# Column 0 in centered form through the first GLU group, rstd applied afterwards, and gate slices 0 to 3 loaded as 128 KB pieces over two queues

## The chip, the cores and the metric

The kernel runs on one core of one Trainium2 chip. The metric is the device time of one execution in microseconds; it was about 1.8 us longer than the span of the profile in the runs that were profiled. Every kernel was run several times, and the kernel before was run in the same rounds on the same chip.

## The reference, cut to what matters

```python
xn = _layernorm(x, axis=-1)                       # x: 1 x 2048 x 512, bf16
return x + _A_ref(xn, A_w_r, A_w_i) + _B_ref(xn, B_w_gate, B_w_up, B_w_down)
# _A_ref: irfft2(rfft2(xn) * (w_r + 1j * w_i))
# _B_ref: (gelu(xn @ w_gate) * (xn @ w_up)) @ w_down, 512 -> 1792 -> 512
```

The 2048 rows are 16 "columns" of 128 tokens, and the 1792 hidden units 14 "slices" of 128.

## The kernel before

All operations are handed to a small planner in the kernel, which simulates the engines with assumed durations (the first number of each call) and fixes the order of the instructions on each engine. TensorE runs dummy matmuls, so that its clock comes up, until the first column is normalised and transposed.

```python
def layernorm(c0, n, due, after=(), halves=1):
    ...                                            # bn_stats, bn_aggr, + eps on DVE
    r = add("POOL", 0.55, lambda: nc.gpsimd.tensor_tensor(
        out=rstd[:, k], in0=ve[:, k], in1=half[:, k], op=ALU.pow), (e, o_mem[1]), due - 5, lag=0.1)
    ...                                            # xn = (x - mean) * rstd on DVE, in halves

def pe_transpose(c, due):
    b = _Buf("S")                                  # one PSUM tile for both halves
    ...
        def ev(es=es, eng=(nc.scalar.copy, V.tensor_copy)[h]):   # half 0 on ACT, half 1 on DVE
            eng(out=xnT[c // 4][:, es[0]:es[-1] + 1, c % 4], in_=tiles[f"tp.{c}"][:, es[0]:es[-1] + 1])

load_x(0, 1); d_ident = load_ct("ident", "ident", "ACT"); load_x(1, 1)
load_w(0, 2, ("SP", "ACT"))                        # gate and up slices 0-1, 256 KB each
load_x(2, 2); load_w(2, 4); load_w(4, 6); load_x(4, 4); load_w(6, 10); load_x(8, 4); load_w(10, 14)
...
FIRST = [(0, 1, 0, 4), (1, 1, 0, 4), (0, 2, 4, 2), (2, 2, 0, 2), (2, 2, 2, 2), (2, 2, 4, 2)]
#        column, columns, slice, slices: one PSUM tile g_ps and one u_ps each
```

## Time and profile before

| | before |
|---|---|
| time, median of 6 runs | 179.50 us (179.39 to 180.25) |
| span of the profile | 177.6 us |
| first GLU matmul | 6.89 us |
| clock of TensorE full from | 7.11 us |
| last matmul starts | 174.70 us |
| last DMA landed, end of the span | 176.71, 177.62 us |

### The profile page before, as it was taken

How to read it: one execution, taken by the hardware profiler on the slowest of the kernel's cores; microseconds unless marked ns; L12 is line 12 of the kernel's file. 1: busy time of each engine (PE TensorE's matmuls, PEld its weight loads, DVE VectorE, ACT ScalarE, POOL GpSimd, SP SyncE). 2: the span in 40 equal slices, each digit the busy share in tenths (PEclk: the TensorE clock that was granted, in tenths of full speed). 3: DMA queues.
4: the chain of work that ended last, by engine and by line, in shares of the span. 5: the costliest groups of instructions: out<-in, count | busy, mean ns of one | idle time of the engine just before them, and what ended most of it. 6: DMA issues, size and time to landing. Idle time of an engine off the chain costs nothing.

```text
span 177.6 us, 3041 instructions
## 1 busy us (share of the span) xinstructions
PE 173.4 (98%) x1100; PEld 92.9 (52%) x1100; DVE 118.1 (66%) x266; ACT 87.4 (49%) x158; POOL 18.6 (10%) x33
## 2 busy tenths in 40 slices
PE   6999999999999999999999999999999999999993
PEld 2598545545554544554555455554445444544463
DVE  1869999999537995889999885336442541632522
ACT  3162437456789737999998855453111211211100
POOL 3212138743200000000000000000000000000000
PEclk9999999999999999999999999999999999999999
DMA  5999487999297001302211121100222221322212
GB/s 144 311 355 359 86 270 84 223 296 193 52 347 255 2 0 29 93 2 59 61 48 37 37 59 37 27 0 0 84 68 66 83 89 59 92 80 69 74 45 59
DMA packets 23182, 19.24 MB, mean 108 GB/s; under 512 B 8512, under 2 KB 21824, under 8 KB 23168
## 3 DMA queue, kind: packets, MB, share of 16 engines
q1 hardware_dynamic: 22176, 17.57, 35.0%
q0 software_dynamic: 320, 1.19, 3.1%
q10 hardware_dynamic: 672, 0.30, 0.6%
q8 instruction: 8, 0.13, 0.3%
q14 instruction: 6, 0.05, 0.1%
HBM read 13.28 MB, written 2.10 MB: 87 GB/s over the span
## 4 chain that ended last, share of the span: by engine, by line
PE 91%; ACT 3%; DVE 3%; issue 1%; POOL 0%; DVEq 0%; POOLq 0%
PE u_ps L502 25%; PE g_ps L502 25%; PE warm L380 3%; ACT E L652 2%; PE yp L818 2%; PE bp L581 2%; PE gp L767 2%; PE yp__2078 L872 2%; PE yp__1994 L872 2%; PE yp__1967 L872 2%; PE yp__1936 L872 2%; PE yp__1909 L872 2%; PE yp__1820 L872 2%; PE yp__1793 L872 2%; PE yp__1762 L872 2%; PE yp__1735 L872 2%
## 5 line engine op out<-in xcount | busy, mean ns | idle before, releaser
L502 PE MATMUL g_ps<-xnT,Wg_sb 128*128 128x512 bf16 (+2 forms) x264 | 58.1, 347 | 0.0
L502 PE MATMUL u_ps<-xnT,Wu_sb 128*128 128x512 bf16 (+2 forms) x264 | 57.9, 347 | 0.0
L527 DVE TENSOR_TENSOR hT<-u_ps,ge 128x512 bf16<-128x512 f32 x56 | 38.4, 685 | 17.5 <-PE u_ps L502 14.4
L519 ACT ACTIVATE ge<-g_ps 128x512 bf16<-128x512 f32 x56 | 33.5, 598 | 30.5 <-PE g_ps L502 26.5
L502 PEld LDWEIGHTS <-Wu_sb 128*128 128x128 bf16 x264 | 24.3, 98 | 22.3 <-DMA Wu_sb<-in_B_w_up_dram 0.2
L502 PEld LDWEIGHTS <-Wg_sb 128*128 128x128 bf16 x264 | 24.3, 98 | 20.7 <-issue 0.2
L872 PEld LDWEIGHTS <-hT 128*128 128x128 bf16 x252 | 23.0, 98 | 21.9
L824 ACT CAST yf<-yp 128x512 bf16<-128x512 f32 x16 | 9.3, 586 | 37.6 <-PE yp L818 37.6
L652 ACT CAST E<-ep 64x512 bf16<-64x512 f32 x32 | 18.5, 579 | 1.1 <-PE ep L646 0.7
L396 DVE BATCH_NORM_STATS2 st<-x_t 128x6 f32<-128x512 bf16 x16 | 10.5, 676 | 4.8 <-DMA x_t<-in_A_x_dram 4.8
L629 ACT CAST ds<-dp 128x512 bf16<-128x512 f32 x16 | 8.8, 589 | 1.1 <-PE dp L624 1.0
L773 ACT CAST Gs<-gp 128x512 bf16<-128x512 f32 x16 | 8.6, 593 | 1.0 <-PE gp L767 1.0
L406 POOL TENSOR_TENSOR rstd<-ve,half 128x2 f32<-128x2 f32 (+2 forms) x7 | 6.6, 949 | 21.9 <-DVE ve L404 21.9
L585 ACT CAST Bs<-bp 128x512 bf16<-128x512 f32 x16 | 8.3, 603 | 0.5 <-PE bp L581 0.5
L818 PEld LDWEIGHTS <-Gs 128*128 128x128 bf16 x64 | 4.8, 98 | 3.5
L380 PE MATMUL warm<-warm 128*128 128x512 bf16 (+1 forms) x14 | 5.1, 539 | 1.3 <-POOL half L373 1.3
L412 DVE TENSOR_SCALAR xn<-x_t,mv,rstd 128x512 bf16<-128x512 bf16 (+1 forms) x17 | 6.1, 399 | 0.3 <-POOL rstd L406 0.3
L818 PE MATMUL yp<-CT,Gs 128*128 128x128 bf16 x64 | 6.0, 219 | 0.0
L683 DVE TENSOR_TENSOR m<-X,TW 128x1024 bf16<-128x1024 bf16 x8 | 5.5, 692 | 0.2
L624 PEld LDWEIGHTS <-Bs 128*128 128x128 bf16 x64 | 4.4, 98 | 2.4
L689 DVE TENSOR_TENSOR m<-X,TW 128x1024 bf16<-128x1024 bf16 x8 | 5.5, 684 | 0.0
L646 PE MATMUL ep<-ds,CT 128*128 128x512 bf16 x16 | 5.4, 379 | 0.0
(103 smaller groups left out, 169.0 us busy)
## 6 DMA issues: line engine op xcount, KB each, us to landing
y<-in_A_x_dram SPq DMA_DIRECT2D x16, 128.0 KB, 2.1
F<-F SPq DMA_DIRECT2D x32, 64.0 KB, 2.0
out_dram<-y SPq DMA_DIRECT2D x15, 128.0 KB, 1.7
Wd_sb<-in_B_w_down_dram SPq DMA_DIRECT2D x2, 896.0 KB, 8.3
x_t<-in_A_x_dram SPq DMA_DIRECT2D x3, 512.0 KB, 6.8
Wg_sb<-in_B_w_gate_dram SPq DMA_DIRECT2D x2, 512.0 KB, 6.8
Wu_sb<-in_B_w_up_dram SPq DMA_DIRECT2D x2, 512.0 KB, 9.1
Wg_sb<-in_B_w_gate_dram SPq DMA_DIRECT2D x3, 256.0 KB, 5.1
```

The costliest lines, as they stand in the source:

```text
L380: nc.tensor.matmul(tiles["warm"][:, 0:w], lhsT=warm[:, 0:P], rhs=warm[:, 0:w], start=True, stop=True)
L396: V.bn_stats(out=st[:], in_=x_t[:, c])
L502: nc.tensor.matmul(tiles[f"{nm}.{key}"][:, f * w:f * w + w], lhsT=W[:, e, (f0 + f) * P:(f0 + f + 1) * P], rhs=rhs(e), start=(f + e == 0), ...
L519: nc.scalar.activation(out=e[:, 0:nf * w], in_=tiles[f"g_ps.{key}"][:, 0:nf * w], func=AF.Gelu_apprx_tanh)
L527: V.tensor_tensor(out=out, in0=tiles[f"u_ps.{key}"][:, 0:nf * w].rearrange("p (f w) -> p f w", w=w) if nf > 1 else tiles[f"u_ps.{key}"][:, ...
L585: nc.scalar.copy(out=o, in_=tiles[f"bp.{cg}.{q}"][:].rearrange("p c (r g a) -> p (c r) g a", r=2, a=4))
L629: nc.scalar.copy(out=ds[:].rearrange("p (s k t) -> p s k t", s=2, t=2), in_=tiles[f"dp.{G}"][:].rearrange("p s t k -> p s k t"))
L652: nc.scalar.copy(out=tiles[f"E.{g}"][64 * h:64 * h + 64, r], in_=tiles[f"ep.{g}.{h}"][64 * r:64 * r + 64])
L773: nc.scalar.copy(out=o, in_=tiles[f"gp.{g}.{h}"][:].rearrange("p q (n a) -> p (q n) a", a=4))
L818: nc.tensor.matmul(yp[:, q], lhsT=tiles["G"][:, q, c], rhs=IQ[q], start=(q == 0), stop=(q == 3), skip_group_check=True)
L824: nc.scalar.copy(out=tiles[f"yf.{c // 2}"][:, c % 2], in_=tiles[f"yp.{c}"][:])
L872: nc.tensor.matmul(y[:, s], lhsT=tiles[sb, f][:, cl * P:(cl + 1) * P], rhs=Wd_sb[:, f, s], start=(f == 0), stop=False)
```

## The change

Its intent is to start the first GLU group before rstd of column 0 is known. The centered x - mean is transposed and multiplied, and the PSUM result is scaled by rstd afterwards. For this rstd must lie along the free axis, so one FP32 matmul of ones with diag(rstd) spreads it. The statistics of columns 1 and 3 move from DVE to ACT (sums by accumulator), to make room on DVE. Each half of a transposed column gets its own PSUM tile. The loads are re-cut with longer rows, and one rule of the planner changes.

```diff
-                    at = max([d.end + d.lag + self.HOP for d in o.deps if d.eng != "PE" or o.eng != "PE"] + [0.0])
+                    at = max([d.end + (0.0 if d.eng == o.eng and not d.nbytes else d.lag + self.HOP)
+                              for d in o.deps if d.eng != "PE" or o.eng != "PE"] + [0.0])
 ...
-    load_w(0, 2, ("SP", "ACT"))
+    d_g = [load_first(e, eng) for e, eng in ((1, "ACT"), (0, "SP"), (3, "ACT"), (2, "SP"))]   # gate 0-3, 128 KB each
 ...
+    d_u = load(NE * P * P * 8, lambda: nc.sync.dma_start(out=Wu_sb[:, :, 0:4 * P], in_=wu_v[:, :, 0:4 * P]))
     load_x(2, 2)
-    load_w(2, 4)
-    load_w(4, 6)
+    load_w(4, 8)
 ...
-    NWARM, NGAP, GAP = 10, 1, 4
+    NWARM, GAP = 7, 2
 ...
+    def glu_first(c, f0, nf):      # g_ps and u_ps from the centered column, then on DVE:
+        def scale(k):
+            V.tensor_tensor(out=sc(k), in0=flat(("g_ps", "u_ps")[k]), in1=R(), op=ALU.mult)
 ...
-    FIRST = [(0, 1, 0, 4), (1, 1, 0, 4), (0, 2, 4, 2), (2, 2, 0, 2), (2, 2, 2, 2), (2, 2, 4, 2)]
+    glu_first(0, 0, 4)
+    FIRST = [(1, 1, 0, 4), (0, 2, 4, 2), (2, 1, 0, 4), (3, 1, 0, 4), (0, 2, 6, 2), (2, 2, 4, 2), (2, 2, 6, 2)]
```

## The prediction

> **What bounds the kernel now.** I read the page first, then the busy time of the engines in three stretches, then the start in order of time. The page, its first part and its chain:
>
> ```profile
> span 177.6 us, 3041 instructions
> ...
> PE 173.4 (98%) x1100; PEld 92.9 (52%) x1100; DVE 118.1 (66%) x266; ACT 87.4 (49%) x158; POOL 18.6 (10%) x33
> ...
> PE 91%; ACT 3%; DVE 3%; issue 1%; POOL 0%; DVEq 0%; POOLq 0%
> ```
>
> TensorE is the bound, but a busy PE can hide slow matmuls, so I cut the span at the first GLU matmul and at the end of the last one (columns: stretch, its length, busy time of each engine with instruction counts, granted clock, DMA share, GB/s):
>
> ```profile
> 6.89:174.80 167.91, 167.78 (x1082) 90.78 (x1081) 115.34 (x257) 85.54 (x155) 15.92 (x23) 1.00 0.38 106
> 0.00:6.89 6.89, 5.52 (x18) 2.10 (x19) 2.45 (x9) 1.86 (x3) 2.67 (x10) 1.00 0.68 201
> ```
>
> The middle is a wall: 167.91 us with 0.13 us idle. From start to start a matmul takes 56 ns with 128 columns, 109 ns with 256 and 216 ns with 512 (medians of the trace's 369, 79 and 651 intervals). The wall has 362, 79 and 641 of them: 362 x 0.056 + 79 x 0.109 + 641 x 0.216 = 167.3 us; all its delays, one of 0.28 us at 75.7 and two of 0.2 us near 7.1 and 8.7 among them, make about 0.5 us. So nothing behind the start can be gained but that half microsecond. What is left is the 6.89 us in front of it:
>
> ```profile
> 1.34 4.45 PE L380 MATMUL warm<-warm 128*128 128x512 bf16 x10 [1.34 <-POOL half L373]
> ...
> 3.51 0.69 DVE L396 BATCH_NORM_STATS2 st<-x_t 128x6 f32<-128x512 bf16 x1 [3.51 <-DMA x_t<-in_A_x_dram]
> 4.23 0.18 DVE L403 BATCH_NORM_AGGREGATE mv<-st 128x2 f32<-128x6 f32 x1
> ...
> 4.76 0.58 POOL L406 TENSOR_TENSOR rstd<-ve,half 128x1 f32<-128x1 f32 x1 [2.70 <-DVE ve L404]
> ...
> 5.38 0.60 DVE L412 TENSOR_SCALAR xn<-x_t,mv,rstd 128x256 bf16<-128x256 bf16 x2
> ...
> 6.23 0.63 PE L380 MATMUL warm<-warm 128*128 128x128 bf16 x4
> 6.47 0.37 ACT L431 COPY xnT<-tp 128x256 bf16<-128x256 bf16 x1 [3.29 <-PE tp L428]
> ...
> 6.88 0.29 DVE L431 COPY xnT<-tp 128x256 bf16<-128x256 bf16 x1 [0.83 <-ACT xnT L431]
> 6.89 0.82 PE L502 MATMUL g_ps<-xnT,Wg_sb 128*128 128x128 bf16 x8
> ...
> 8.00 0.39 PE L428 MATMUL tp<-CT,xn 128*128 128x128 bf16 x4
> ```
>
> Here is a serial chain: x lands, statistics, pow on GpSimd, normalise, transpose, copy, first GLU matmul. The two copies of one PSUM tile also run one behind the other (0.83 us of wait in the DVE line).
>
> **What the Trainium skill says.** "TensorE: Matmul & The Clock Gate", section "What's actually happening": an idle TensorE runs at half clock until a free-running window of about 3.4 us has been busy. The trace agrees: the ten dummies span 4.45 us, which is 427 ns apart; four 128-column ones span 0.63 us at 6.23 (107 ns apart) and four transposes 0.39 us at 8.00 (56 ns). The switch to full clock falls at 7.11 us in this run. The section "Wait — 56ns, not 53.3ns?" has 55.6 and 215.7 ns, as here. "FP8 and Floating Point Precision", section "TensorE Precision Notes": true FP32 takes four passes; the new FP32 matmul should then cost about 4 x 56 ns; nothing in before shows it. "DMA: Bandwidth & Descriptors", section "Issuing engines are not separate DMA queues": a second issuing engine saves only issue time. The trace fits: the up piece issued by ACT took 4.2 us to land, those of SP 5.1 to 5.9.
>
> **The change part by part.**
>
> 1. Start. The mean is out at 4.42; centring needs no rstd. By the old spacing (first half 0.35 us, second 0.26 later) the centred halves are ready at 4.80 and 5.06, their transposes start at about 4.85 and 5.11. Each half now has its own PSUM tile: transpose end about 5.24, DVE copy 5.28 to 5.57, first GLU matmul 5.6. The four cold dummies behind the second half (5.30 + 4 x 0.107) end at 5.73, so I take 5.73 instead of 6.89: 1.16 us earlier. The second half's copy (0.37 us on ACT, from about 5.54) is ready for it in time.
> 2. Weights. Gate pieces of 128 KB bring the same 800 KB by the same point as before, when the gate piece landed at 5.85; with 1 KB instead of 512 B rows I put the first two pieces near 4.9 and the others near 5.5. The second half of the gate needs them at about 6.5. The 512 KB up piece: 1312 KB had landed at 7.88 before; at the 356 GB/s of the 9 to 13 us stretch I estimate 7.2, needed at 8.0. Hidden.
> 3. Half clock. The earlier matmuls run before 7.11. From 5.73 to 7.11 some 13 matmuls at 107 ns do what takes 0.72 us warm: 0.66 us lost of the 1.16. Before lost about 0.06. The window is free-running, so this differs from run to run: nothing lost if the clock switches by 5.7, over 1 us if at 8. It may be why one of the three runs of before took 180.25 and the others 179.4 and 179.5.
> 4. More PE work. By the order of the built program the wall has 430 + 1 matmuls of 128 columns, 79 of 256 and 625 of 512. Slices 0-3 of columns 2 and 3 turn from 32 of 256 into 64 of 128 (+0.10 us); slices 6 and 7 of block 0 from 16 of 512 into 32 of 256 (+0.03); column 0 is transposed a second time, behind the first GLU matmuls (+4 x 0.056 = 0.22); the FP32 matmul that spreads rstd (+0.22, perhaps 0.3). Sum +0.6 us.
> 5. Beside it: two scalings of 128x512 out of PSUM (0.69 us each, like hT) and the diagonal on DVE, against the statistics of columns 1 and 3 (0.69 + 0.18 each) that go to ACT as two 0.6 to 0.7 us passes. DVE stays even, and its work is behind PE, which has two PSUM buffers each for gate and up.
> 6. Later: the x load of columns 2 and 3 now follows the up piece (estimate 8.1 instead of 6.73), so normalised columns 2 and 3 come at about 11.1 and 12.0; PE asks for them at 11.6 and 12.7. The three gathers of w_r go ahead of the rstd of columns 4 and 5 on GpSimd: they took 4.8 us with gaps (27.36 to 32.18) before, so from about 11.5 to 16.3. DVE then waits for this rstd with up products queued behind it; their buffer is due to PE at about 19. My estimate of both is 0.1 to 0.3 us of stalls.
>
> Sum: -1.16 + 0.60 (half clock, net) + 0.60 + 0.2 = +0.2 us. Against it the 0.5 us of old delays can partly go: the up weights waited for at 8.8 come earlier, and the order is new, so the 0.28 us at 75.7 may fall out (-0.4 us). With a switch before 7.11, which most phases of a 3.4 us window give, the loss in 3 shrinks to 0.4 on average (-0.2 us). I end at -0.3 to -0.4 us: 179.52 becomes 179.2.
>
> **Rivals.** (a) The start is worth its full 1.2 us: the clock switches early and the stalls vanish. For it: the wall is dense, so a shift of its start moves its end. Against: the 7.11 us of this trace and the counted 0.6 us of work. It would give 178.6. (b) A wait takes the place of the one removed: fewer dummies (7 wide and 6 narrow for 10 and 4) and a hole at 4.5 to 4.85 delay the clock by a window, or DVE, stuck behind the rstd after the gathers, holds an up buffer at 19 us for 0.7 us. For it: DVE is at 2.00 us of 2.00 in the stretches from 14 to 20 us. Against: before too had holes around 5.7 and 6.8 and switched. It would give 180 to 180.5. (c) The gate pieces land late, as small transfers share the 16 engines, and the first matmuls wait up to 0.5 us: largely swallowed by the cold clock; 179.4.
>
> **Range and chances.** The wall cannot shrink, so a gain of 2% (3.6 us) would need the start at about 3.3 us, before x has landed; a loss of 2% needs several new stalls. Both get 1%. The range runs from rival (a) to rival (b): 178.4 to 180.1.
>
> **What would show it.** First g_ps matmul at 5.6 to 5.8; matmuls 107 ns apart up to the switch; one FP32 matmul of 0.2 to 0.3 us; a wall of about 168 us to the last matmul at 174.3 to 174.6. I am wrong if the first GLU matmul is later than 6.3, if PE shows gaps over 0.5 us in sum between 8 and 22 us, or if the last matmul comes before 173.8 or after 175.4.

## More of the kernel before

The studies fell on four chips, on which the kernel before had medians of 179.36, 179.48, 179.28 and 180.07 us, so a kernel is compared with the kernel before of its own rounds.

The prediction shows the page and the start. For the comparison I also cut the span in three (columns: stretch, its length, busy time of each engine with its instructions, granted clock, DMA share, GB/s):

```profile
0.00:15.00 15.00, 13.61 (x126) 9.56 (x127) 8.79 (x24) 5.81 (x10) 3.38 (x11) 1.00 0.91 283
15.00:50.00 35.00, 35.00 (x231) 19.52 (x230) 31.43 (x72) 18.61 (x34) 15.21 (x22) 1.00 0.79 191
50.00:178.00 128.00, 124.80 (x748) 63.80 (x745) 77.86 (x172) 62.98 (x114) 0.00 (x0) 1.00 0.22 65
```

In the middle stretch TensorE, the first number with a count, is busy 35.00 of 35.00 us. So every new wait of TensorE there would lengthen the kernel, and none can be removed.

## The result, and the profile after

The changed kernel took 180.72 us in the median of 6 runs (180.15 to 181.20), against 179.50 us before in the same rounds. The ratio is 1.0059, with a 95% interval of 1.0033 to 1.0086. A ratio here is the mean time of one kernel's runs over that of the other's of the same rounds, so it is not quite the ratio of the medians. For e1 to e16 the ratios come out when the first run of each kernel, the profiled one, is left out. The change is within 2%, as predicted, but the range of 178.4 to 180.1 us is missed, and the sign of the small change is wrong.

The page of the changed kernel (span, busy times, chain by engine):

```profile
span 178.9 us, 3167 instructions
...
PE 173.0 (97%) x1153; PEld 95.0 (53%) x1153; DVE 119.7 (67%) x269; ACT 90.8 (51%) x168; POOL 17.5 (10%) x35
...
PE 73%; DVE 16%; DMA 3%; issue 2%; POOL 2%; SPq 1%
```

TensorE is busy 0.4 us less in a span that is 1.3 us longer, and the chain of waits runs for 16% of the span over DVE and for 3% over DMA, where it had been TensorE for 91%. The same three stretches of the changed kernel:

```profile
0.00:15.00 15.00, 12.69 (x135) 9.67 (x136) 8.89 (x25) 9.02 (x20) 6.26 (x15) 1.00 0.90 296
15.00:50.00 35.00, 34.60 (x269) 20.96 (x266) 33.11 (x73) 17.17 (x32) 11.21 (x20) 1.00 0.77 172
50.00:178.00 128.00, 125.74 (x756) 64.35 (x753) 77.70 (x172) 64.65 (x118) 0.00 (x0) 1.00 0.23 69
```

The idle time of TensorE lies in the first 15 us and, with 0.40 us, in the second stretch. In the last one it is busier only because more work was left. The start of the changed kernel, in order of time:

```profile
4.97 0.29 DVE L497 COPY scr_w<-tm 128x256 bf16<-128x256 bf16 x1 [0.25 <-PE tm L494]
5.10 0.72 ACT L423 ACTIVATE xn<-x_t,sm 128x512 bf16<-128x512 bf16 x1
...
5.32 0.61 PE L578 MATMUL g_ps<-scr_w,Wg_sb 128*128 128x128 bf16 x8
...
5.82 0.35 ACT L497 COPY scr_w<-tm 128x256 bf16<-128x256 bf16 x1
...
6.22 0.61 PE L578 MATMUL g_ps<-scr_w,Wg_sb 128*128 128x128 bf16 x8 [0.29 <-ACT scr_w L497]
...
9.32 0.69 DVE L407 BATCH_NORM_STATS2 st<-x_t 128x6 f32<-128x512 bf16 x1 [1.19 <-DMA x_t<-in_A_x_dram]
...
10.34 0.68 DVE L598 TENSOR_TENSOR scr_b<-g_ps,scr_r 128x512 f32<-128x512 f32 x1
...
11.14 0.78 PEld L630 LDWEIGHTS <-Wg_sb 128*128 128x128 bf16 x8 [0.82 <-DMA Wg_sb<-in_B_w_gate_dram]
11.17 1.03 PE L630 MATMUL g_ps<-xnT,Wg_sb 128*128 128x256 bf16 x8 [0.68 <-DVE scr_b L598]
```

The reader should see four things. The first GLU matmul starts at 5.32 us, 1.57 us earlier than before. Its second half waits for an ACT copy, which stands behind the accumulating passes over column 1 (the second of them at 5.10); this stops TensorE for 0.46 us. And at 9.32 us DVE takes the statistics of column 2, for whose x it has waited 1.19 us; the scaling of g_ps, ready long before, stands behind them in DVE's order. So the first gate buffer comes free at 11.02, and TensorE stops for 0.84 us at 10.3. And the gate slices that it needs next, 4 and 5, come with a load that landed at 10.82 (the PEld line, the weight load). So two waits lie nearly on top of each other: with the buffer free TensorE could have gone on at about 10.87, only some 0.3 us earlier. This is an estimate, from the landing and the 0.05 us that passed in e8_split_dve from a landing at 8.12 to the matmul at 8.17.

To add this up I took, for each matmul, the time to the start of the next and subtracted the spacing of its width (56, 109 or 216 ns, as in the prediction); what is left are the gaps. A small negative sum is rounding of those three numbers. The FP32 matmul, which the trace records twice, is counted as four of 128 columns. The terms add up to the spans:

| us | before | after | difference |
|---|---|---|---|
| start of the first GLU matmul | 6.89 | 5.32 | -1.57 |
| work at the three spacings | 167.30 | 167.87 | +0.57 |
| gaps before 15 us | 0.40 | 1.72 | +1.32 |
| gaps 15 to 50 us | -0.04 | 0.72 | +0.76 |
| gaps after 50 us | 0.14 | -0.10 | -0.24 |
| last matmul start to last DMA landed | 2.01 | 2.01 | 0.00 |
| last DMA landed to end | 0.91 | 1.34 | +0.43 |
| sum | 177.6 | 178.9 | +1.3 |

The gaps of 15 to 50 us are two, in front of and inside the third of the four bp groups, at 44 us. The changed kernel there (several engines):

```profile
39.04 1.38 POOL L433 TENSOR_TENSOR rstd<-ve,half 128x4 f32<-128x4 f32 x1 [11.50 <-DVE ve L415]
...
43.56 0.68 DVE L692 TENSOR_TENSOR xf<-A 128x1024 bf16<-128x1024 bf16 x1
44.16 0.68 DVE L696 TENSOR_TENSOR xf<-A 128x1024 bf16<-128x1024 bf16 x1
...
44.29 0.40 PE L710 MATMUL bp<-RF_t,xf 128*128 128x128 bf16 x4 [0.20 <-DVE xf L692]
44.89 0.84 PE L710 MATMUL bp<-RF_t,xf 128*128 128x128 bf16 x12 [0.20 <-DVE xf L696]
```

TensorE gets xf from DVE at the last moment. The line of GpSimd shows why the planner may have thought it early: pow on 128x4 takes 1.38 us, and the planner has 0.55 us for it.

For the end, the waits of SyncE (waited for: us in total, times, longest); first before, then after:

```profile
SPq L922 <- DMA out_dram<-y: 0.6, 1, 0.6
```

```profile
SPq L1058 <- DMA out_dram<-y: 1.0, 1, 1.0
```

At the end SyncE waits for the completion semaphores of the DMAs in a fixed order, with eight instructions about 62 ns apart. Before, the last store counted on one that the last of them waits for. After, with another number of DMAs, it counts on one of the first, and the seven others follow the landing: 7 x 62 ns is the 0.43 us of the table.

### The profile page after: what moved, and what is told of

It reads as the page before. It is cut to its first block, busy times and chain, and to the rows that moved or that the text cites.

```text
span 178.9 us, 3167 instructions
## 1 busy us (share of the span) xinstructions
PE 173.0 (97%) x1153; PEld 95.0 (53%) x1153; DVE 119.7 (67%) x269; ACT 90.8 (51%) x168; POOL 17.5 (10%) x35
## 3 DMA queue, kind: packets, MB, share of 16 engines
q0 software_dynamic: 320, 1.19, 2.8%
## 4 chain that ended last, share of the span: by engine, by line
PE 73%; DVE 16%; DMA 3%; issue 2%; POOL 2%; SPq 1%
PE u_ps L630 18%; PE g_ps L630 17%; DVE st L407 5%; DVE hT L655 4%; DMA x_t<-in_A_x_dram 3%; DVE xn L439 2%; PE gp L898 2%; PE dp L755 2%; PE yp L954 2%; PE ep L777 2%; PE yp__2122 L1008 2%; PE yp__2095 L1008 2%; PE yp__2064 L1008 2%; PE yp__1979 L1008 2%; PE yp__1948 L1008 2%
## 5 line engine op out<-in xcount | busy, mean ns | idle before, releaser
L630 PE MATMUL g_ps<-xnT,Wg_sb 128*128 128x512 bf16 (+2 forms) x272 | 56.4, 338 | 0.7 <-DVE scr_b L598 0.7
L630 PE MATMUL u_ps<-xnT,Wu_sb 128*128 128x512 bf16 (+2 forms) x272 | 56.4, 338 | 0.0
L655 DVE TENSOR_TENSOR hT<-u_ps,ge 128x512 bf16<-128x512 f32 x55 | 37.5, 683 | 15.3 <-PE u_ps L630 13.4
L647 ACT ACTIVATE ge<-g_ps 128x512 bf16<-128x512 f32 x55 | 33.0, 601 | 28.6 <-PE g_ps L630 27.1
L407 DVE BATCH_NORM_STATS2 st<-x_t 128x6 f32<-128x512 bf16 x14 | 9.4, 674 | 4.4 <-DMA x_t<-in_A_x_dram 4.4
L433 POOL TENSOR_TENSOR rstd<-ve,half 128x1 f32<-128x1 f32 (+2 forms) x7 | 6.1, 865 | 21.4 <-DVE ve L415 19.9
L898 PEld LDWEIGHTS <-F 128*128 128x128 bf16 x64 | 4.2, 98 | 1.9
L439 DVE TENSOR_SCALAR xn<-x_t,mv,rstd 128x512 bf16<-128x512 bf16 x13 | 4.8, 408 | 0.6 <-POOL rstd L433 0.6
L391 PE MATMUL warm<-warm 128*128 128x512 bf16 (+1 forms) x13 | 3.9, 470 | 1.3 <-POOL half L383 1.3
## 6 DMA issues: line engine op xcount, KB each, us to landing
Wu_sb<-in_B_w_up_dram SPq DMA_DIRECT2D x2, 384.0 KB, 10.3
```

The costliest lines, as they stand in the source:

```text
L407: V.bn_stats(out=st[:], in_=x_t[:, c])
L630: nc.tensor.matmul(tiles[f"{nm}.{key}"][:, f * w:f * w + w], lhsT=W[:, e, (f0 + f) * P:(f0 + f + 1) * P], rhs=rhs(e), start=(f + e == 0), ...
L647: nc.scalar.activation(out=e[:, 0:nf * w], in_=tiles[f"g_ps.{key}"][:, 0:nf * w], func=AF.Gelu_apprx_tanh)
L655: V.tensor_tensor(out=out, in0=tiles[f"u_ps.{key}"][:, 0:nf * w].rearrange("p (f w) -> p f w", w=w) if nf > 1 else tiles[f"u_ps.{key}"][:, ...
```

## The experiments

Sixteen kernels ran, in four batches: e1 to e4, e5 to e8, e9 to e11 with e13, and e12 with e14 to e16. The theories, where an expectation uses a letter: T, the late x load of columns 2 and 3 makes the gap at 10.3 us; S, the first 15 us are bound by what has landed, so that what is gained at one wait is given back at the next; P, the planner's duration of pow makes the bp gaps. The table has the measured values; "sum" is start plus gaps before 15 us, and "end" is last landing to end.

| kernel | median us | ratio to before [95%] | start | gaps <15 | sum | gaps 15-50 | end |
|---|---|---|---|---|---|---|---|
| before | 179.50 | | 6.89 | 0.40 | 7.29 | -0.04 | 0.91 |
| after | 180.72 | 1.0059 [1.0033, 1.0086] | 5.32 | 1.72 | 7.04 | 0.72 | 1.34 |
| e1_swap | 181.11 | 1.0101 [1.0084, 1.0117] | 5.37 | 2.51 | 7.88 | 0.38 | 1.34 |
| e2_tail | 180.56 | 1.0058 [1.0036, 1.0081] | 5.37 | 1.94 | 7.31 | 0.75 | 0.91 |
| e3_dve | 180.43 | 1.0068 [1.0046, 1.0091] | 5.17 | 1.71 | 6.88 | 1.03 | 1.34 |
| e4_sched | 179.87 | 1.0032 [1.0016, 1.0049] | 6.72 | 0.49 | 7.21 | 0.95 | 0.91 |
| e5_loads | 180.39 | 1.0058 [1.0023, 1.0093] | 6.50 | 0.71 | 7.21 | -0.03 | 1.34 |
| e6_pow | 180.23 | 1.0025 [0.9989, 1.0061] | 5.40 | 1.72 | 7.12 | 0.18 | 1.34 |
| e7_split | 180.21 | 1.0044 [1.0005, 1.0083] | 5.37 | 1.49 | 6.86 | 0.69 | 1.21 |
| e8_split_dve | 180.49 | 1.0048 [1.0020, 1.0075] | 5.66 | 1.34 | 7.00 | 0.81 | 1.21 |
| e9_all | 179.38 | 1.0009 [0.9988, 1.0030] | 5.36 | 1.36 | 6.72 | 0.31 | 0.91 |
| e10_landed | 180.39 | 1.0063 [1.0021, 1.0104] | 5.37 | 1.53 | 6.90 | 0.82 | 1.34 |
| e11_landed_dve | 180.53 | 1.0071 [1.0045, 1.0097] | 5.22 | 1.34 | 6.56 | 0.81 | 1.34 |
| e13_halves | 179.34 | 1.0001 [0.9983, 1.0020] | 6.25 | 0.87 | 7.12 | -0.04 | 0.91 |
| e12_math | 184.44 | 1.0217 [1.0173, 1.0260] | 5.99 | 2.38 | 8.37 | 2.27 | 0.91 |
| e14_pow_tail | 180.20 | 0.9999 [0.9960, 1.0038] | 5.96 | 1.11 | 7.07 | 0.50 | 0.91 |
| e15_again | 181.19 | 1.0048 [1.0010, 1.0087] | 6.04 | 2.02 | 8.06 | 1.56 | 1.34 |
| e16_base | 179.87 | 0.9982 [0.9936, 1.0028] | 7.08 | 0.26 | 7.34 | 1.94 | 0.91 |

The terms come from one profile each, while the time of one kernel varied by 0.2 to 2.2 us between runs; so a ratio shows a whole, and a profile shows where. The profiled runs of e15 and e16 were the slowest of their six, those of e4 and e5 the fastest of their four. In the profiles of e1 to e4 some 15 matmul records are missing, which I bridged. Gaps before 15 us hold cold matmuls too: in e1 and e6 the clock came up only at 7.14 and 7.33 us, which is about 0.8 us of their gaps (16 matmuls at 107 ns instead of 56).

### The x load of columns 2 and 3 goes first: e1_swap

```diff
+    i, j = order.index(d_u), order.index(XD[2])       # the 512 KB up load and the x load
+    order[i], order[j] = XD[2], d_u
```

> The changed kernel with one thing different: the x load of columns 2 and 3 is issued in front of the 512 KB up load instead of behind it; every other instruction keeps its place. Theory T (late x blocks VectorE in order, and VectorE then holds the gate buffer and runs late up to the folds): x of columns 2 and 3 lands about 1 us or more earlier than 9.30, the 0.84 us gap of TensorE near 10.3 shrinks to at most 0.5 us, the two gaps of 0.36 us near 44 shrink too, the up load lands some 0.7 us later and may open a gap of up to 0.4 us near 7.6; in sum 0.6 to 1.1 us faster than the changed kernel (about 179.8). Rival W (the gate slices 4 to 7, landing at 10.82, set the gap): the gap near 10.3 stays at 0.5 us or more and the total moves by less than 0.3 us.

The x load landed at 7.08 instead of 9.30 us and the gap at 10.3 us was gone. But the up load, now behind it, landed at 9.39, and this line of the start of e1_swap appeared:

```profile
9.44 1.07 PE L578 MATMUL u_ps<-scr_w,Wu_sb 128*128 128x128 bf16 x16 [1.44 <-DMA Wu_sb<-in_B_w_up_dram]
```

The kernel became slower. T falls as a recipe: with x early the gate buffer was free at 9.93 instead of 11.02 us, but putting x first only moves the wait, and makes it longer. That the gap at 10.3 is gone proves little here, as TensorE now comes there only at 12.1 us.

### One load of W_down, so that the last DMA counts on the last semaphore: e2_tail

```diff
-        nc.sync.dma_start(out=tiles["Wd"][:, 7 * k:7 * k + 7], in_=wd_v[:, 7 * k:7 * k + 7])
+            nc.sync.dma_start(out=tiles["Wd"][:], in_=wd_v)          # once
```

> The changed kernel with the two down-weight loads made one, so that one DMA fewer is issued and the last output lands on the last of the eight DMA semaphores instead of the first. Theory E (the end of the program waits for the eight semaphores one after the other, 62 ns each, and in the changed kernel all eight come behind the last landing): the time from the last landing to the end falls from 1.34 to about 0.9 us, and the kernel is 0.43 us faster (about 180.3) with the work in front unchanged. Rival: the difference of the ends is chance, and the time stays within 0.15 us.

The end went from 1.34 to 0.91 us, as expected. The total did not show it: in that profile the gap at 10.2 us was 1.22 instead of 0.84 us, with the x load landing at 9.59. A term of 0.4 us is lost in the variation of the start; it takes e14 to see it.

### DVE scales before it takes the statistics of column 2: e3_dve

```diff
+    late = seq[k:k + 3]        # statistics of column 2 and what follows from them, moved behind the scalings
+    order[at:at] = late
```

> The changed kernel with the loads as they are, but on VectorE the statistics of column 2 (three instructions, and their pow on GpSimd) stand behind the two scalings of column 0 instead of in front of them. Theory T: the scaling of the gate product starts near 8.3 instead of 10.34, so the gate buffer is free long before TensorE asks; the gap near 10.3 falls from 0.84 to what the gate slices 4 to 7 leave, about 0.5 us, and the later chain on VectorE gains as well: 0.3 to 0.9 us faster. Rival W (weights alone): 0.3 us at most.

The gap at 10.3 us was gone, but this profile alone doesn't show that the order did it. The up load landed at 8.00 us and TensorE waited 0.65 us for it at 7.4; so it asked for the buffer only at 10.74, when the gate slices 4 to 7 had landed too (10.65). With x landing at 8.95 in this run, the old order would have freed the buffer at about 10.7 as well (an estimate: in the changed kernel the scaling ended 1.72 us after x landed). e10 and e11 below separate the two. Another 0.37 us was a wait for normalised column 2 at 11.6. The ratio is not better than that of the unmended kernel.

### The parts alone, put into the kernel before: e4_sched and e5_loads

e4 takes over only the planner rule, and e5 only the list of loads with its four gate pieces; the diffs are against the kernel before.

```diff
-                    at = max([d.end + d.lag + self.HOP for d in o.deps ...])                        # e4_sched
+                    at = max([d.end + (0.0 if d.eng == o.eng and not d.nbytes else d.lag + self.HOP) ...])
```

```diff
-    load_w(0, 2, ("SP", "ACT"))                                                                     # e5_loads
+    d_g = [load_first(e, eng) for e, eng in ((1, "ACT"), (0, "SP"), (3, "ACT"), (2, "SP"))]
+    d_u = load(...)                    # up 0-3; then x 2-3, weights 4-7, x 4-7, weights 8-10, x 8-11, weights 11-13
```

> The kernel before with nothing but the new rule of its planner (no assumed delay between dependent instructions of one engine). If the loss of the changed kernel came from the new order of instructions that this rule makes, this kernel is 0.5 us or more slower than before; if the rule is harmless, it is within 0.3 us of before.

> The kernel before with nothing but the new list of loads (gate slices 0 to 3 in four 128 KB pieces over two queues, one 512 KB up load, x of columns 2 and 3 behind it, later slices in larger loads); the mathematics of column 0 as before. Theory S (what the weights and x supply, not the chain of column 0, sets the time once columns 0 and 1 are used up): the first GLU matmul stays at 6.7 to 6.9, x of columns 2 and 3 lands near 9 instead of 6.7, TensorE waits for their transposes or for slices 4 and 5 by 0.5 to 1.5 us between 8 and 13, and the kernel is 0.5 to 1.2 us slower than before (180.0 to 180.6). If the loads are harmless and the loss lies in the new mathematics, it is within 0.3 us of before.

The rule alone costs 0.3% (0.57 us, as its theory asked), and it alone brings the two bp gaps into the old kernel (the start of bp in e4_sched):

```profile
41.96 0.40 PE L582 MATMUL bp<-RF_t,xf 128*128 128x128 bf16 x4 [0.21 <-DVE xf L564]
42.56 0.84 PE L582 MATMUL bp<-RF_t,xf 128*128 128x128 bf16 x12 [0.20 <-DVE xf L568]
```

It removes a safety margin between operations of one engine; where another duration is assumed too short, this margin had hidden it. The loads alone cost 0.6%, about 1.0 us, as S said, but the profile shows only 0.4 us of it: the start came 0.39 us earlier, the gaps grew by 0.31 us and the end by 0.43. The waits that S named between 8 and 13 us are not there, with x landing at 8.47; this profiled run was the fastest of the four, and what the others lost was not seen. The new list is thus no faster for the old arithmetic.

### The planner gets the measured duration of pow: e6_pow

```diff
-        r = add("POOL", 0.55, lambda: nc.gpsimd.tensor_tensor(
+        r = add("POOL", (0, 0.55, 0.7, 0, 1.4)[n], lambda: nc.gpsimd.tensor_tensor(
```

> The changed kernel with one number of its planner changed: the pow on GpSimd is planned at 0.55, 0.7 and 1.4 us for 1, 2 and 4 columns, as the trace shows it, instead of 0.55 for all. Theory P (the new rule took away padding that had hidden this, so the folds' matmuls stand too early in TensorE's order): the two gaps of 0.36 us near 44 vanish and the kernel is 0.5 to 0.7 us faster than the changed one (ratio to before near 1.002). Rival (the folds are late because VectorE lost 1 us at 9.3): the gaps stay.

Both bp gaps are gone, only 0.18 us are left from 15 to 50 us, and the ratio falls from 1.0059 to 1.0025, though the intervals of these two overlap. P holds: the rule lets the planner trust its durations, and the one of pow was wrong.

### Slices 4 to 7 in pairs, alone and with DVE's order: e7_split and e8_split_dve

```diff
+                h, d = (a + b) // 2, nc.sync.dma_start      # gate 4-5, up 4-5, gate 6-7, up 6-7
+                d(out=t[:, :, a:h], in_=v[:, :, a:h])
+                d(out=Wg_sb[:, :, h:b], in_=wg_v[:, :, h:b])
+                d(out=t[:, :, h:b], in_=v[:, :, h:b])
```

> The changed kernel with gate and up slices 4 to 7 loaded as slices 4 and 5, then 6 and 7 (four loads of 256 KB for two of 512 KB), engine orders unchanged. Theory S: the gate slices 4 and 5 land about 0.6 us earlier (near 10.1), but the gap near 10.3 stays over 0.5 us, since VectorE, held by x of columns 2 and 3, still has the gate buffer; together the kernel gains less than 0.4 us. Rival W (the size of that load alone): the gap falls to 0.2 us or less and the kernel gains 0.6 us or more.

> The same split of slices 4 to 7, and the statistics of column 2 behind the scalings on VectorE. Theory S: the gate buffer and the slices 4 and 5 are both there, so the gap near 10.3 is under 0.2 us; what remains are waits for the up load near 7.4 (0 to 0.7 us, as it lands) and for x of columns 2 and 3 before their transposes near 12 (up to 0.4 us); 0.5 to 1.0 us faster than the changed kernel. If waits only move, so that the sum of TensorE's gaps between 5 and 15 us stays at 1.5 us or more, the supply as a whole is the bound there.

In e7 the gap at 10.3 us is gone, which S had not expected, and one of 0.79 us at 7.6 stands in its place, with the up load landing at 8.36; TensorE came to the next gate group only at 11.1, when buffer and weights were there. In e8 TensorE waits 0.60 us at 6.1 for a gate piece that landed at 6.75, and 0.37 us at 11.7 for normalised column 2; the 0.5 to 1.0 us expected of it did not come (ratio 1.0048 against 1.0059). The sums of 6.86 and 7.00 us hardly differ from the 7.04 of the changed kernel.

### An earlier start alone, in the kernel before: e13_halves

```diff
-                if h == 0:
-                    psum(f"tp.{c}", [P, NE, P], BF16)
+                psum(f"tp.{c}.{h}", [P, NE, P], BF16)     # and an own buffer, so that ACT and DVE copy side by side
```

> The kernel before, with one thing of the change: each transposed half of a column has its own PSUM tile, so that the ACT copy and the VectorE copy run side by side. Loads, planner and work are as before. The first GLU matmul should start at about 6.5 to 6.6 instead of 6.89. If an earlier start is worth its size, the kernel is 0.3 us faster than before (ratio 0.998). Theory S says that the weights of the first stages, which land no earlier, take it back: start plus gaps before 15 us stays at 7.2 to 7.3 us, ratio 0.999 to 1.001.

This is the cleanest test, as it has the old loads, the old work and the old planner. The first GLU matmul starts 0.64 us earlier, and the time is the same (1.0001; the interval's lower end, 0.9983, just excludes the 0.998 of a start worth 0.3 us). Not all of the 0.64 us is the edit's: in this profile x of column 0 landed 0.36 us earlier than before (3.12 against 3.48), and the clock was full from 5.42 instead of 7.11. The start of e13_halves shows where it went:

```profile
6.25 0.61 PE L501 MATMUL g_ps<-xnT,Wg_sb 128*128 128x128 bf16 x8
...
7.77 0.62 PE L501 MATMUL g_ps<-xnT,Wg_sb 128*128 128x128 bf16 x8 [0.25 <-DMA Wg_sb<-in_B_w_gate_dram]
...
8.67 0.62 PE L501 MATMUL u_ps<-xnT,Wu_sb 128*128 128x128 bf16 x8 [0.28 <-DMA Wu_sb<-in_B_w_up_dram]
```

TensorE now waits for slices 2 and 3; from start to start these two gaps are 0.41 and 0.45 us, where all gaps before 15 us had been 0.40 us. Of the 0.64 us 0.47 are given back. The kernel before was thus already within about 0.2 us of its supply.

### Weights that have landed: e10_landed and e11_landed_dve

```diff
-        for k, nm, W, tag, b in (..., (1, "u_ps", Wu_sb, "U", ub)):
+        for k, nm, W, tag, b in (..., (1, "u_ps", Wg_sb, "U", ub)):       # first group only
+        fe = 4 if (c0, n) == (0, 2) else 0                                # slices 4-7 of columns 0, 1 read 0-3
```

e11 has DVE's order of e3 as well. The result is wrong; the comparison with the reference passed it nevertheless, so its tolerance doesn't cover these products.

> Wrong result on purpose: the changed kernel, but the first u_ps groups and the groups of slices 4 to 7 of columns 0 and 1 read gate slices 0 to 3, which have landed long before, so that TensorE no longer waits for the up load or for slices 4 to 7. All DMAs stay. Theory S: start plus gaps before 15 us fall from 7.0 by 0.3 us or more, with the wait for Wu gone and the part of the 10.3 us gap that the scaling on VectorE causes (about 0.7 us) left; total 0.2 to 0.5 us below the changed kernel in the same rounds or runs. Rival: the gap at 10.3 us is VectorE's alone, then gaps stay at 1.7 and the time at 180.5 to 180.8.

> Wrong result on purpose: the same reading of landed slices, and the statistics of column 2 behind the two scalings on VectorE. Now neither the landings of weights nor the buffer of the scaling can hold TensorE before 15 us; left are the second half of column 0 (0.46 us), the small ones around the FP32 matmul (0.3 us in sum) and the wait for normalised columns 2 and 3. Theory S: start plus gaps before 15 us at most 6.5 us (each of the two mends alone gave back its gain, together they don't), total 179.8 to 180.2. If it stays near 7.0 us, something other than weights and scaling bounds these 15 us, the x load of columns 2 and 3 most likely.

The waits for weights are gone, but in e10 the DVE wait of the start remains:

```profile
11.04 1.05 PE L631 MATMUL g_ps<-xnT,Wg_sb 128*128 128x256 bf16 x8 [0.43 <-DVE scr_b L598]
```

Its sum is 6.90, a fall of only 0.14 us, which is a miss for S. With DVE's order mended too (e11) this gap is gone, and TensorE is not later than in e10:

```profile
10.42 1.04 PE L631 MATMUL g_ps<-xnT,Wg_sb 128*128 128x256 bf16 x8
```

The two differ in DVE's order alone, and this group needs no late weights in either. So DVE's order does hold the buffer, and costs 0.59 us of TensorE where weights don't. The sum of e11 is 6.56, just over what S allowed; 0.63 us at 5.7 (ACT's copy) and 0.38 us at 11.3 (column 2) remain. Neither total was distinguishable from the changed kernel's, and S's 179.8 to 180.2 us for e11 is missed. So the landing of weights isn't the one bound. Weights, ACT's copy, DVE's order and the x load lie within about half a microsecond of each other, and mending one or two of them uncovers the next.

### Everything mended: e9_all

This is the changed kernel with the edits of e6, e7 and e3, and with W_down in seven loads, so that the last store counts on the last semaphore.

```diff
-        nc.sync.dma_start(out=tiles["Wd"][:, 7 * k:7 * k + 7], in_=wd_v[:, 7 * k:7 * k + 7])
+        for a, b in (((0, 2), (2, 4), (4, 6), (6, 7)), ((7, 9), (9, 11), (11, 14)))[k]:
+            nc.sync.dma_start(out=tiles["Wd"][:, a:b], in_=wd_v[:, a:b])
```

> The changed kernel with four mends at once: the planner's duration of pow by width, gate and up slices 4 to 7 loaded in pairs, VectorE's statistics of column 2 behind the two scalings, and W_down in seven pieces so that the last DMA of the program falls on the lane that SyncE waits for last. If each of the stalls named (scaling order 0.7 us, the two gaps in front of bp 0.7 us, 0.4 us at the end) is worth its size, 1.2 to 1.8 us come off: 178.9 to 179.5, even with the kernel before or a little faster. Theory S (the first 15 us are bound by what has landed, so that an earlier start and fewer stalls are given back as waits for weights) says that only the bp gaps and the end come off, about 0.5 to 0.9 us: 179.8 to 180.2, with start plus gaps before 15 us still 6.9 to 7.3 us.

At 179.38 us it is 0.9 us better by the ratios (1.0009 against 1.0059). The total lies in the range of the other reading, 178.9 to 179.5, and below S's; but the gain of 0.9 us is the top of S's 0.5 to 0.9 and short of the other's 1.2 to 1.8, since the kernel before was 0.2 us faster in these rounds too. So this run decides for neither, and its sum of 6.72 is just below S's. By its ledger 0.41 us come from the bp gaps, 0.43 from the end and 0.32 from start and gaps. Against the kernel before, the sum of start and gaps is 0.57 us better, which is what the added work costs; so both are equal.

### Again in the same rounds: e15_again, e16_base, e14_pow_tail, e12_math

e15 and e16 are the two kernels unedited, for second profiles. e14 is the changed kernel with e6 and e2. e12 is the changed kernel with the load list of the kernel before:

```diff
-    d_g = [load_first(e, eng) for e, eng in ((1, "ACT"), (0, "SP"), (3, "ACT"), (2, "SP"))]
+    load_w(0, 2, ("SP", "ACT"))
...
-    load_w(4, 8)
+    load_w(2, 4)
+    load_w(4, 6)
```

> The changed kernel unedited, for a second profile and as the base of the others in these rounds: ratio to before 1.005 to 1.008. If the ledger of the first profile is right, the second has the two gaps of 0.36 us in front of bp and 1.34 us from the last landing to the end again, and start plus gaps before 15 us at 6.9 to 7.3 us, whatever its parts are.

> The kernel before, unedited, for a second profile and as a control: ratio 0.999 to 1.001; start plus gaps before 15 us 7.2 to 7.3 us, no gap in front of bp, 0.91 us from the last landing to the end.

> The changed kernel with the planner's duration of pow by width and W_down in one load, which puts the last DMA on the last lane: the bp gaps (0.7 us) and 0.4 us at the end should go, and nothing at the start. If the ledger is right: 0.7 to 1.1 us below e15_again, ratio to before 1.000 to 1.003. If these two were only put down to the loss, it stays within 0.3 us of e15_again.

> The changed kernel's arithmetic and order with the load list of before. The first group of column 0 needs slices 0 to 3 of both weights, which then land at 7.9 and 8.8 us in pairs, so TensorE waits for them: start plus gaps before 15 us 7.5 us or more, and at least 0.3 us slower than e15_again. If instead start plus gaps stays at 7.0 us, the new load list buys nothing and the wait is made elsewhere.

On this chip all was slower and more variable: even e16 had 1.94 us of gaps between 36 and 44 us, where TensorE waited for hT and xf from DVE, 0.81 us of it inside a bp group, against the expectation; a late DVE can thus open such gaps without the new rule too. e15 repeats the two bp gaps (0.41 and 0.37 us) and the 1.34 us at the end; its profiled run was the slowest of its six, with x of columns 2 and 3 landing at 10.32 us, a gap of 1.53 us at 10.6 and a sum of 8.06, above what I had expected. The two small mends of e14 take 0.5% off e15 (0.9999 against 1.0048), about 0.9 us, within the 0.7 to 1.1 expected. The intervals of the two ratios overlap; compared directly, the means of the five runs after the first are 180.31 and 181.19 us, 0.89 us apart with a 95% interval of about 0.2 to 1.6 worked out from these runs, so the gain is clear and its size is not. In e14 the bp group at 44 us stands in one line:

```profile
44.50 1.06 PE L710 MATMUL bp<-RF_t,xf 128*128 128x128 bf16 x16
```

e12 is the slowest of all, 1.7% over e15. It needs slices 0 to 3 of the gate for column 0 at once, and has them late (the start of e12_math):

```profile
7.70 0.84 PE L572 MATMUL g_ps<-scr_w,Wg_sb 128*128 128x128 bf16 x12 [1.31 <-DMA Wg_sb<-in_B_w_gate_dram]
```

So the new arithmetic needs the new list. Another 2.27 us of gaps after 15 us, among them 1.29 us at 21, are of its other order and say nothing on the question.

## Why the prediction was wrong

Its picture of the bound was right, and so was most of the working on the start; the waits that follow the start were mis-sized, and the end was left out. By its steps:

1. **Start (-1.16).** It came out larger, -1.57 us in the first profiles and -1.04 in the second ones (7.08 to 6.04). In the first, x of column 0 landed at 3.21 instead of 3.48 us. But "The second half's copy [...] is ready for it in time" failed: it was put at 5.54, began at 5.82 behind the statistics that had moved to ACT, and TensorE, at full clock already, waited 0.46 us for it.
2. **Weights ("Hidden").** One reading was wrong: "the up piece issued by ACT took 4.2 us to land, those of SP 5.1 to 5.9". The first gate piece, issued by SP, took 4.2 us as well, and SP's later pieces 5.2 to 6.2, so these two pieces show no difference between the engines. The gate pieces landed at 4.49 to 5.65 us, near the estimates. The up load landed at 7.09, just in time, in the first profile, but at up to 8.36 in the eleven others that have this order of loads. TensorE asks for it at about 7.6. So it was hidden in the first profile, in e2 and in e9, and waited for 0.17 to 0.79 us in e3, e7, e8 and e15.
3. **Half clock (+0.60).** It cost nothing in the first profile: the clock came up at 5.19 us. In all profiles the switch lies between 3.98 and 7.33, so this is the phase that the prediction spoke of.
4. **More work (+0.6).** Right: 0.57 us in the ledger, and 0.30 us for the FP32 matmul until the next start.
5. **"DVE stays even, and its work is behind PE, which has two PSUM buffers each for gate and up."** This step failed. DVE's busy time did stay nearly even (118.1 and 119.7 us), but busy time doesn't tell the order. The scaling stood behind statistics that waited for a DMA, and so it held a PSUM buffer until 11.02 us; TensorE stopped for 0.84 us at 10.3. Some 0.3 us of these are DVE's alone, as the gate slices landed at 10.82. e10 and e11, which don't need these slices and differ in DVE's order only, show the step by itself: 0.59 us, and no gap.
6. **"My estimate of both is 0.1 to 0.3 us of stalls."** This is the term that was mis-sized most: the gaps before 15 us grew by 1.32 us. The x load was put at 8.1 us from the mean rate. Of its 16 parts the eighth landed at 7.47 and the fifteenth at 8.32 us, but the last at 9.30, and the consumer waits for the last. The Trainium skill, "DMA: Bandwidth & Descriptors", section "Why a DMA increments its semaphore by 16 and not by 1", says that the engines finish independently and that only the full 16 means landed; the trace agrees. In twelve profiles with the new list this load's last part came 0.9 to 2.5 us after its eighth; with the old list the same load had 0.4 to 0.6 us, and the up load of slices 2 and 3, which landed at about the same time, 0.4 to 0.9. The gathers that the step feared delayed nothing; the wait at 19 us didn't come.

The rest of the sum: "the 0.5 us of old delays can partly go (-0.4 us)". The 0.28 us at 75.7 did go, and -0.24 us is measured. But the new order brought two delays of its own, 0.76 us in front of and in bp, which e4 traces to the planner rule and e6 to the duration of pow. The prediction did not speak of this rule's effect at all, nor of the end, where another count of DMAs costs 0.43 us (e2, e5, e14).

Rival (b), "a wait takes the place of the one removed", had the right direction and the right engine, but the wrong place: a gate buffer at 10.3 us behind the x load, not an up buffer at 19 behind the gathers. What the start gains is nearly all given back in the first 15 us: the sum of start and gaps is 7.29 us before and 7.04 after (7.34 and 8.06 in the second profiles, where more than the gain was lost), and e13 shows the same in the kernel before with nothing else changed. The remaining 0.25 us of the first profiles do not pay for the 0.57 us of work; bp and the end add the rest.

Open are three things. Why the last part of a load lags more with the new list is not settled: between 6.2 and 8.7 us no DMA packet took over 150 ns before, and 17 of them did after, up to 669 ns, but no run tells what stalls them. And the share of each of the coupled waits before 15 us can't be given singly, since removing one changes the others. Nor does any total show what these gaps cost: e3, e8, e10 and e11 stand at 1.0048 to 1.0071 against 1.0059 for the changed kernel, though the sum of e11 is 0.48 us lower. No version measurably beat the kernel before; e9, e13 and e14 equal it.

## What to carry to other kernels

In this kernel an earlier start was worth only the slack to the next input: before moving one, list when each following load's last part lands and when it is asked for, because the mean rate is too kind. If a moved operation holds a buffer, look at what stands before it in its engine's order, not at how busy the engine is. After any change of a planner's rule or of the number of DMAs, check the places that the change doesn't mention, here a duration planned 0.8 us too short and the order of the waits at the end; together they cost 1.19 us, about three times the gain of 0.3 to 0.4 us that was predicted. And when a gap vanishes in an experiment, check that the engine did not just come later.

## What the Trainium skill lacked or had wrong

- "DMA: Bandwidth & Descriptors" says that the parts of a DMA finish independently, but has no figure for how far apart: here, from the eighth to the last part of one 256 KB load of x, 0.4 to 0.6 us with one list of loads, and 0.9 to 2.5 us with the other, which brings the same bytes in fewer and larger loads after four small pieces.
- "FP8 and Floating Point Precision", section "TensorE Precision Notes", has four passes for true FP32, but no duration. The trace shows two records for the one FP32 matmul of 128x128, 0.30 us from its start to the next matmul's, so the cost of about four 128-column matmuls plus 0.08 us agrees, while the count of passes can't be seen.
- "GPSIMD Engine Reference" has no duration for pow: here 0.58 us for 128x1 and 1.38 us for 128x4 in the changed kernel, far from flat in the width, and 1.98 and 1.04 us for the two of 128x4 in the kernel before, so not fixed either.
- No page tells of the waits for the DMAs' completion at the end of a program: about 62 ns for each of eight instructions, so 0.91 or 1.34 us from the last landing to the end, by the semaphore that the last store counts on.
